# Attention in front of two MoE layers on one core: scores ahead of the v products, earlier stores of x, moved weight splits

## The chip, the cores and the metric

The kernel runs on one core of a Trainium2 chip, in one launch. The metric is the device time of that launch in microseconds. Names of engines: PE is TensorE, DVE VectorE, ACT ScalarE, POOL GpSimd, and SP the engine that issues the loads and stores (SPq its DMA queue). A round or a tile is given by its number n, a layer of the program by its name.

## What is computed

A recurrent attention with a decay w per head and channel, over 4 batches, 8 heads of 48 channels and 768 steps, feeds a mixture of 8 experts (one expert per token), and that a second, dense layer with the function h − tanh(h).

```python
def _attn_ref(r, k, v, w, u):                    # r, k, v: 4, 8, 768, 48
    for t in range(S):
        cur = np.einsum('bhd,bhe->bhde', u[None] * kt, vt)
        y[:, :, t] = np.einsum('bhd,bhde->bhe', rt, state + cur)
        state = w[None, :, :, None] * state + np.einsum('bhd,bhe->bhde', kt, vt)

def _moe_ref(x, w_gate, w1, w2):                 # x: 3072 x 384, F 1024
    expert_idx = np.argmax(x @ w_gate, axis=1)   # gate_w: its softmax value
    out[mask] = gate_w[mask, None] * (np.maximum(x[mask] @ w1[e], 0.0) @ w2[e])

def _moe2_ref(x, w_in, w_out):                   # 384 x 2048, 2048 x 384
    h = x @ w_in
    return (h - np.tanh(h)) @ w_out
```

## The kernel before

The attention is cut into 24 tiles of 128 steps: 6 chunks c of the sequence, 4 batches b in each, tile n = 4c + b. The loop `for n in range(NN + 1)` runs a round for each tile and one more. The order of the instructions on each engine is the order in which the program writes them; nothing reorders them later. Loads run three tiles ahead into five buffers (`t_b` holds r and k by channel, `n_b` holds r, k, v by step).

A round n does this. VectorE: `diag_sum(n+1)` (dt, L356) reduces GpSimd's product rku; `scale(n+1)` (L328) multiplies the two halves of t by tables of powers of w, one of them in PSUM (prkK) and the other, from tile 4 on, in SBUF (PRK); `mask(n)` (L377) copies the scores that lie below the diagonal from PSUM into `am`; `state_add(n)` (L402) adds the new keys' products to the state Sc. TensorE: the product of the state with tile n−1 (L418) and of `am` with its values (L423, "v products", both in `outp(n-1)`), the products for the state (`state_mm`, L390), and `scores(n)` (L372), which go into two PSUM banks A0 and A1, of which there is one pair. ScalarE: the copies of y (L428) and `diag(n+1)` (L363, eight parts), which writes the diagonal of `am` from dt. GpSimd: `side(n+2)` with the products rk (L336) and rku (L342), `side_kh(n+2)` (L351), whose keys only the state products use, and sw (L401).

Every fourth round has a piece of the routing for a whole chunk besides: `logits(c)` in round 4c+5 (lps on TensorE, lt on ScalarE), `gate` one round later, `rank_of`, `rank_in` (ohh, ol) and `rank_q` (hv on GpSimd) after that, then `idx_mm` and idf. Once a tile's gate is known, `xout_t` turns it back to rows of tokens (Xps, L570) and `xout_g` scales it on ScalarE (xs, L577) and stores it to xd. Xps and lps share one PSUM bank, "X", until round 23, when a second joins it. `XOUT` says which tiles leave in which round where that isn't n−7; in a list of two, the second follows the scores.

Between these stand the first weights of the MoE: `LOADS` says in which round a weight is loaded, `SPLITS` in which it is split into two parts for the matmuls: a cast on ScalarE (L84), then a subtraction on VectorE (L85). `head_end` (L492, five small VectorE operations) counts the first 256 tokens of expert 0 among chunks 0 to 3, that is tiles 0 to 15; `head_gather` (L597) fetches their rows from xd by the indices idxh with two indirect DMAs, and `head_trans` (L610) transposes them on TensorE behind the last v products. A barrier follows, and then the two MoE layers.

Of the kernel before, what the change touches and what calls it, by code (L numbers as in the profile page):

```python
# [8 lines left out]
F32 = mybir.dt.float32  # L9
# [5 lines left out]
ACTF = mybir.ActivationFunctionType  # L15
# [15 lines left out]
def rwkv_moe_moe_kernel(ctx: ExitStack, tc: tile.TileContext, rk_t, rkv, pk, u, wp1, wp2, out):  # L31


    nc = tc.nc
    B, C, P, _, H, D = rkv.shape
    N, DM = out.shape
    NT = N // P
    HP = H // 2
# [14 lines left out]
    H0 = C - 2  # L53
# [293 lines left out]
        side_rku(n)  # L347

    def side_kh(n):
        kh = kh_b[n % 3]  # L350
        nc.gpsimd.tensor_tensor(out=kh[:, R0:].rearrange("p (h d) -> p h d", d=D), in0=n_b[n % NB][:, 1], in1=KT, op=ALU.mult)  # L351
        st["kh", n] = kh
# [3 lines left out]
        nc.vector.tensor_reduce(out=dt, in_=st.pop(("rku", n)), axis=AX.X, op=ALU.add)  # L356
        st["dt", n] = dt

    def diag(n):
        dt = st.pop(("dt", n))  # L360
        am = at3.tile([P, 2, HP, P], F32, tag="am", name="am")
        for h in range(H):
            nc.scalar.activation(out=am[:, h % 2, h // 2, :], in_=ident, func=ACTF.Copy, scale=dt[:, h:h + 1])  # L363
        st["am", n] = am

    def scores(n):
        t = t_b[n % NB]
        ps = [ps1.tile([P, HP, P], F32, tag=f"A{q}", name=f"A{q}") for q in range(2)]
        for j in range(HP):
            for q in range(2):  # L370
                rows = slice(64, PT) if q else slice(0, 64)
                nc.tensor.matmul(ps[q][:, j, :], lhsT=t[rows, 1, j, :], rhs=t[rows, 0, j, :], start=True, stop=True)  # L372
        st["A", n] = ps

    def mask(n):
        for q, ps in enumerate(st.pop(("A", n))):
            nc.vector.copy_predicated(out=st["am", n][:, q],  # L377
                                      mask=mlt.bitcast(U32).unsqueeze(1).to_broadcast([P, HP, P]),
                                      data=ps)
# [25 lines left out]
        state_mm(n)  # L405
        state_add(n)

    def outp(n):
        c, b = seq[n]
        am = st.pop(("am", n))  # L410

        if c > 0:
            for i in range(2):
                for g in range(2):
                    for q in range(2):
                        rows = slice(64, PT) if q else slice(0, 64)
                        j, p0 = 2 * i + g, 64 * g
                        nc.tensor.matmul(Yp[q][p0:p0 + D, i, :], lhsT=Sc[c % 2][b][rows, j, :],  # L418
                                         rhs=t_b[n % NB][rows, 0, j, :], start=(i == 0), stop=False)
        for q in range(2):  # L420
            for j in range(HP):
                i, p0 = j // 2, 64 * (j % 2)
                nc.tensor.matmul(Yp[q][p0:p0 + D, i, :], lhsT=n_b[n % NB][:, 2, 2 * j + q, :],  # L423
                                 rhs=am[:, q, j, :], start=(c == 0 and i == 0), stop=(i == 1))
        if b == 0:
            st["y", c] = yp.tile([P, HP, B, P], F32, tag="y", name="y")
        for q in range(2):
            nc.scalar.copy(out=st["y", c].rearrange("p (q i) b t -> p q i b t", q=2)[:, q, :, b, :], in_=Yp[q])  # L428
# [280 lines left out]
    with tc.manual_schedule():  # L709
# [36 lines left out]
        k_table()  # L746
        side(1)
        nc.gpsimd.memset(cum[0], 0.0)
        LAG = 7
        L = C - 1  # L750
        LOADS = {5: (0, 0), 9: (0, 1), 13: (1, 0), 15: (1, 1), 17: (2, 0), 20: (2, 1), NN - 1: (3, 0)}
        SPLITS = {8: (0, 0), 12: (0, 1), 16: (0, 2), 18: (0, 3), **{NN - 3 + k: (1, k) for k in range(3)}}
        LATER = {0: ((3, 0), (3, 1)), 1: ((2, 2), (2, 3)), 2: ((3, 2), (3, 3))}
        XOUT = {NN - 3: (NN - 10, NN - 9), NN - 2: (), NN - 1: (NN - 8, NN - 7), NN: ()}
        for n in range(NN + 1):
            if n == NN:
                w_split(1, 3)
                w_split(2, 0)
                w_split(2, 1)
            if n + 3 < NN:  # L760
                load(n + 3)
            if n in LOADS:
                w_load(*LOADS[n])
            if n + 1 < NN:
                diag_sum(n + 1)
                scale(n + 1)
            at_step(n, 2, logits)
            at_step(n, 6, rank_q)
            xs_of = [m for m in XOUT.get(n, (n - LAG,)) if m >= 0]
            with_logits = n % B == 1 and n > B  # L770
            if n == NN - 1:
                st["both"] = True
            if xs_of and not with_logits:
                xout_t(xs_of[0])
            if 1 <= n <= NN:
                outp(n - 1)
                at_step(n, 6, rank_row)
            if n > 1 and n < NN:
                state_mm(n)
            if xs_of and with_logits:  # L780
                xout_t(xs_of[0])
            if xs_of:
                xout_g(xs_of[0])
            if 0 < n < NN - 1:
                diag(n + 1)
            if n < NN:
                scores(n)
                for m in xs_of[1:]:
                    xout_t(m)
                    xout_g(m)  # L790
                mask(n)
                if n == 0:
                    k_rows()
                    diag(1)
                elif n == 1:
                    state(0)
                    state(1)
                else:
                    state_add(n)
            if n + 2 < NN:  # L800
                side(n + 2)
                if n == 0:
                    side_kh(0)
                    side_kh(1)
                side_kh(n + 2)
            at_step(n, 3, logits2)
            at_step(n, 3, gate)
            at_step(n, 6, idx_mm)
            if n == H0 * B + 3:
                head_count()  # L810
            at_step(n, 4, rank_mm)
            at_step(n, 4, rank_of)
            at_step(n, 5, rank_in)
            if n == H0 * B + 3:
                head_end()
            if n == NN - 2:
                head_gather()
            if n == 0:
                keep_warm(8)
                gate_rows()  # L820
            if n == 1:
                scale_rows()
                gate_cols()
                nc.vector.tensor_reduce(out=nok, in_=ok, axis=AX.X, op=ALU.add)
                nc.vector.memset(one, 1.0)
            if n == 3:
                range_flag(ok)
                nc.vector.tensor_copy(out=e8p, in_=e8)
                nc.vector.tensor_copy(out=thp, in_=thr)
                for t in exs:  # L830
                    nc.vector.memset(t[:, :, E:E + 1], 1e-9)
                nc.vector.tensor_reduce(out=sel, in_=ident.rearrange("p (j x) -> p x j", j=HP)[:, 0:E, :],
                                        axis=AX.X, op=ALU.add)
            if n in SPLITS:
                w_split(*SPLITS[n])

# [675 lines left out]
```

## Time and profile before

| What | us |
|---|---|
| median of 3 runs (lowest, highest) | 772.84 (772.15, 774.85) |
| the profiled execution | 772.78 |
| span of its trace | 771.1 |
| PE busy in the span | 755.7 (98%) |
| DVE busy | 639.2 (83%) |
| ACT busy | 509.1 (66%) |
| POOL busy | 430.9 (56%) |

The profile is of one execution. Times in its rows are counted from the start of the span; what is outside it is 1.7 us. A row of the timeline gives the start, the duration, the engine and the line, the output and inputs, how many instructions were joined in the row, and in brackets how long the engine had been idle before and what ended that. The attention part ends at about 131 us.

### The profile page before, as it was taken

To read this page: it belongs to the slowest core of one execution; us is meant where nothing else is said; L and a number is where in the kernel's file an instruction comes from. 1 tells how busy PE (TensorE), PEld (TensorE's weight loads), DVE (VectorE), ACT (ScalarE), POOL (GpSimd) and SP (SyncE) were. 2 spreads that over 40 slices of the span, in tenths; PEclk is the share of its full clock that TensorE was granted. 3 is DMA by queue.
4 is the path that set the end of the run, shared out by engine and by line. 5 is a ranking of instruction groups with operands and counts; after the bars stand their busy time and mean duration, and the time that the engine had idled before them with its cause. 6 is when DMAs were issued, how large, how long until landed. Compare 5 with 4: busy or idle time off the path is not lost.

```text
span 771.1 us, 14624 instructions
## 1 busy us (share of the span) xinstructions
PE 755.7 (98%) x5200; PEld 684.6 (89%) x5200; DVE 639.2 (83%) x1155; ACT 509.1 (66%) x1091; POOL 430.9 (56%) x435
## 2 busy tenths in 40 slices
PE   8899989999999999999999999999999999999997
PEld 7688868998999999999898998989989989899887
DVE  7899996788899888964898888888888888888893
ACT  6788885464454445554887766776777677677881
POOL 6989952385877876765355353443534344343433
PEclk9999999999999999999999999999999999999999
DMA  8999945466999899974000010000001000000101
GB/s 238 261 291 290 318 128 167 145 189 201 256 230 271 223 305 286 250 198 144 1 1 0 1 42 1 0 21 21 1 1 42 1 1 24 18 1 1 41 1 42
DMA packets 34656, 89.67 MB, mean 116 GB/s; under 512 B 5499, under 2 KB 12704, under 8 KB 34578
## 3 DMA queue, kind: packets, MB, share of 16 engines
q1 hardware_dynamic: 30384, 78.68, 34.8%
q0 software_dynamic: 4192, 9.99, 4.6%
q8 instruction: 43, 0.70, 0.4%
q14 instruction: 35, 0.29, 0.1%
q10 hardware_dynamic: 2, 0.00, 0.0%
HBM read 72.92 MB, written 15.74 MB: 115 GB/s over the span
## 4 chain that ended last, share of the span: by engine, by line
PE 51%; issue 2%; ACT 1%; POOL 1%; POOLq 0%
PE h L1346 25%; PE o L1394 24%; PE y L1119 1%; PE hps L1094 1%; POOL out_dram L1407 0%; PE o L1346 0%; POOL g L1383 0%; POOLq L1453 0%; POOL xb L1383 0%; ACT s L1354 0%; ACT mk L1356 0%; POOLq L1507 0%; ACT xb L1382 0%; ACT z L1350 0%; ACT t L1352 0%
## 5 line engine op out<-in xcount | busy, mean ns | idle before, releaser
L1383 POOL TENSOR_TENSOR g<-t,g 128x512 fp32r<-128x512 f32 x93 | 120.3, 1294 | 178.6 <-ACT g L1382 128.5
L1346 PE MATMUL h<-xb,ring 128*128 128x512 f32 x855 | 213.6, 395 | 0.0
L1394 PE MATMUL o<-ring,g 128*128 128x384 f32 x1116 | 209.3, 336 | 0.0
L1394 PEld LDWEIGHTS o<-ring,g 128*128 128x128 f32 x1116 | 196.1, 188 | 8.2
L1346 PEld LDWEIGHTS h<-xb,ring 128*128 128x128 f32 x855 | 159.7, 188 | 30.5
L85 POOL TENSOR_TENSOR ring<-stg,ring 128x384 fp32r<-128x384 f32 x102 | 105.3, 1053 | 53.8 <-ACT ring L84 42.4
L1350 ACT ACTIVATE z<-h 128x512 f32<-128x512 f32 x95 | 56.9, 599 | 95.2 <-PE h L1346 95.2
L1119 PE MATMUL y<-h,ring 128*128 128x256 f32 (+7 forms) x576 | 114.2, 342 | 0.6 <-DVE h L1098 0.6
L1094 PE MATMUL hps<-xt,ring 128*128 128x472 f32 (+6 forms) x504 | 105.6, 353 | 0.1
L1119 PEld LDWEIGHTS y<-h,ring 128*128 128x128 f32 x576 | 101.3, 188 | 4.1 <-DVE h L1098 1.0
L1362 DVE TENSOR_TENSOR t<-t,h 128x512 f32<-128x512 f32 x95 | 65.1, 685 | 41.3 <-ACT t L1352 40.9
L1094 PEld LDWEIGHTS hps<-xt,ring 128*128 128x128 f32 x504 | 90.6, 188 | 3.7 <-DVEq L1233 0.4
L1367 DVE COPY_PREDICATED t<-mk,h 128x512 f32<-128x512 uint32 x95 | 71.4, 751 | 10.1 <-DVE h L1365 0.5
L84 ACT CAST ring<-stg 128x384 fp32r<-128x384 f32 x152 | 70.2, 512 | 9.5 <-DMA stg<-in_wp_dram 8.9
L1364 DVE SCALAR_TENSOR_TENSOR h<-s,h 128x512 f32<-128x512 f32 x95 | 66.2, 697 | 10.6 <-ACT g L1382 0.9
L1097 ACT ACTIVATE h<-hps 128x256 fp32r<-128x256 f32 (+7 forms) x64 | 32.1, 501 | 63.8 <-PE hps L1094 61.8
L1354 ACT ACTIVATE s<-z,gb 128x512 f32<-128x512 f32 x96 | 69.6, 725 | 0.0
L1356 ACT ACTIVATE mk<-z,gt 128x512 f32<-128x512 f32 x96 | 69.3, 721 | 0.0
L1365 DVE SCALAR_TENSOR_TENSOR h<-z,h 128x512 f32<-128x512 f32 x95 | 66.1, 696 | 3.3
L1363 DVE TENSOR_TENSOR h<-h,z 128x512 f32<-128x512 f32 x95 | 65.9, 693 | 0.0
L1382 ACT CAST g<-t 128x512 fp32r<-128x512 f32 x93 | 57.6, 619 | 9.7 <-DVE t L1367 7.8
L363 ACT ACTIVATE am<-ident,dt 128x128 f32<-128x128 f32 x192 | 58.6, 392 | 3.8 <-DVE dt L356 3.8
(254 smaller groups left out, 1039.6 us busy)
## 6 DMA issues: line engine op xcount, KB each, us to landing
stg<-in_wp_dram SPq DMA_DIRECT2D x64, 384.0 KB, 4.9
n<-in_rkv_dram SPq DMA_DIRECT2D x24, 576.0 KB, 6.0
d<-in_wp_dram SPq DMA_DIRECT2D x32, 384.0 KB, 5.8
t<-in_rk_t_dram SPq DMA_DIRECT2D x24, 384.0 KB, 7.1
wdec<-dcf SPq DMA_DIRECT2D x32, 192.0 KB, 5.3
xd<-xs SPq DMA_DIRECT2D x24, 192.0 KB, 3.9
stg<-wdec SPq DMA_DIRECT2D x12, 384.0 KB, 4.3
wl<-wdec SPq DMA_DIRECT2D x2, 768.0 KB, 6.0
```

Of the source, the lines that this page charges most:

```text
L84: nc.scalar.copy(out=dst[:, 0, sl], in_=of)
L85: eng.tensor_tensor(out=dst[:, 1, sl], in0=of, in1=dst[:, 0, sl].bitcast(F32), op=ALU.subtract)
L1094: nc.tensor.matmul(ps, lhsT=wf(a, kk), rhs=xt[e][b][:, kk, :], start=(n == 0), stop=(n == 8))
L1119: nc.tensor.matmul(yps[d], lhsT=wf(a)[:, d * P:(d + 1) * P], rhs=h2[:, b, :], start=(f == 0 and n == 0), stop=(f == CH1 - 1 and n == 2))
L1346: nc.tensor.matmul(ps, lhsT=wf(a, kk), rhs=xb[j][:, b, kk, :], start=(n == 0), stop=(n == 8))
L1354: nc.scalar.activation(out=s, in_=z, func=ACTF.Square, scale=G_K ** 0.5, bias=gb)
L1356: nc.scalar.activation(out=mk, in_=z, func=ACTF.Relu, scale=-1.0, bias=gt2)
L1364: nc.vector.scalar_tensor_tensor(out=ps, in0=s, scalar=G_K * G_D, in1=ps, op0=ALU.add, op1=ALU.mult)
L1365: nc.vector.scalar_tensor_tensor(out=ps, in0=z, scalar=G_A, in1=ps, op0=ALU.subtract, op1=ALU.mult)
L1367: nc.vector.copy_predicated(out=t, mask=mk.bitcast(U32), data=ps)
L1383: nc.gpsimd.tensor_tensor(out=g[:, 1, :], in0=ww, in1=g[:, 0, :].bitcast(F32), op=ALU.subtract)
L1394: nc.tensor.matmul(ops[q], lhsT=gg[i][:, b, q * P:(q + 1) * P], rhs=wf(a), start=(f == 0 and n == 0), stop=(f == CH2 - 1 and n == 2))
```

## The change

- Rounds 0 to 4 (`AHEAD = B + 1`): `scores(n)` and `mask(n)` stand ahead of the v products of tile n−1, and five of the eight parts of `diag(n+1)` ahead of the copies of y. `outp` is divided for it into `outp_state` and `outp`.
- `side_kh` returns at once for the last chunk, tiles 20 to 23.
- `SPLITS`: (0,0), (0,1), (0,2) one round later; (0,3) and (1,0) on GpSimd, in rounds 20 and 21.
- `XOUT`: tiles 12 and 13 leave in round 19, 14 and 15 in round 20.
- `head_end` in round 21 instead of 19; the load (2,1) in round 21 instead of 20.

```diff
     def side_kh(n):
+        if seq[n][0] == C - 1:
+            return
-    def diag(n):
-        dt = st.pop(("dt", n))
-        am = at3.tile([P, 2, HP, P], F32, tag="am", name="am")
-        for h in range(H):
-            nc.scalar.activation(out=am[:, h % 2, h // 2, :], in_=ident, func=ACTF.Copy, scale=dt[:, h:h + 1])
-        st["am", n] = am
+    def diag(n, part=range(H)):
+        if 0 in part:
+            st["am", n] = at3.tile([P, 2, HP, P], F32, tag="am", name="am")
+        dt, am = st["dt", n], st["am", n]
+        for q, j in (divmod(k, HP) for k in part):
+            h = 2 * j + q
+            nc.scalar.activation(out=am[:, q, j, :], in_=ident, func=ACTF.Copy, scale=dt[:, h:h + 1])
-        LAG = 7
+        LAG, AHEAD = 7, B + 1
-        LOADS = {5: (0, 0), 9: (0, 1), 13: (1, 0), 15: (1, 1), 17: (2, 0), 20: (2, 1), NN - 1: (3, 0)}
-        SPLITS = {8: (0, 0), 12: (0, 1), 16: (0, 2), 18: (0, 3), **{NN - 3 + k: (1, k) for k in range(3)}}
+        LOADS = {5: (0, 0), 9: (0, 1), 13: (1, 0), 15: (1, 1), 17: (2, 0), 21: (2, 1), NN - 1: (3, 0)}
+        SPLITS = {9: (0, 0), 13: (0, 1), 17: (0, 2), 20: (0, 3, nc.gpsimd), 21: (1, 0, nc.gpsimd), 22: (1, 1), 23: (1, 2)}
-        XOUT = {NN - 3: (NN - 10, NN - 9), NN - 2: (), NN - 1: (NN - 8, NN - 7), NN: ()}
+        XOUT = {NN - 5: (NN - 12, NN - 11), NN - 4: (NN - 10, NN - 9), NN - 3: (), NN - 2: (), NN - 1: (NN - 8, NN - 7), NN: ()}
...
-            if 1 <= n <= NN:
+            if n:
+                outp_state(n - 1)
+            if n < AHEAD:
+                scores(n)
+                mask(n)
+                if n:
+                    diag(n + 1, range(5))
+            if n:
                 outp(n - 1)
...
-                diag(n + 1)
+                diag(n + 1, range(5 if n < AHEAD else 0, H))
             if n < NN:
-                scores(n)
+                if n >= AHEAD:
+                    scores(n)
                 for m in xs_of[1:]:
                     xout_t(m)
                     xout_g(m)
-                mask(n)
+                if n >= AHEAD:
+                    mask(n)
...
-            if n == H0 * B + 3:
+            if n == NN - 3:
                 head_end()
```

TensorE, round 4 and the start of round 5, before (A_569 and A_570 are the scores of tile 4, `am,n_133` the v products of tile 3, kh_159 the state products of tile 4, lps the logits of chunk 0; repeated rows left out):

```order
L423 MATMUL yh_161<-am,n_133 48x128 x4
L423 MATMUL yh_162<-am,n_133 48x128 x4
L390 MATMUL yh_163<-n_134,kh_159 64x48
...
L372 MATMUL A_569<-t_129 128x128
L372 MATMUL A_570<-t_129 128x128
...
L452 MATMUL lps<-y,wgp 32x512 x4
```

The same place in the changed kernel, where the scores are A_542 and A_543:

```order
L375 MATMUL A_542<-t_129 128x128
L375 MATMUL A_543<-t_129 128x128
...
L428 MATMUL yh_161<-am,n_133 48x128 x4
L428 MATMUL yh_162<-am,n_133 48x128 x4
L393 MATMUL yh_163<-n_134,kh_159 64x48
...
L457 MATMUL lps<-y,wgp 32x512 x4
```

The scores of tile 4 moved from behind the state products to the head of the round; the logits follow the round as before.

ScalarE, rounds 20 and 21, before (xs is x of a tile, am the eight diagonals, lt the logits, rh a piece of the ranks):

```order
L428 COPY y<-yh_162 128x2x128
L577 ACTIVATE xs<-Xps,gt 128x384
L363 ACTIVATE am<-ident,dt 128x128 x8
L455 COPY lt<-lps 128x512
L428 COPY y<-yh_161 128x2x128
L428 COPY y<-yh_162 128x2x128
L546 ACTIVATE rh<-hv,pid 128x4x32
L577 ACTIVATE xs<-Xps,gt 128x384
L363 ACTIVATE am<-ident,dt 128x128 x8
L577 ACTIVATE xs<-Xps,gt 128x384
L84 CAST ring_70<-stg 128x384
```

The same rounds in the changed kernel:

```order
L433 COPY y<-yh_162 128x2x128
L582 ACTIVATE xs<-Xps,gt 128x384
L367 ACTIVATE am<-ident,dt 128x128 x8
L582 ACTIVATE xs<-Xps,gt 128x384
L84 CAST ring_69<-stg 128x384
L460 COPY lt<-lps 128x512
L433 COPY y<-yh_161 128x2x128
L433 COPY y<-yh_162 128x2x128
L551 ACTIVATE rh<-hv,pid 128x4x32
L367 ACTIVATE am<-ident,dt 128x128 x8
L84 CAST ring_70<-stg 128x384
```

Round 20 now has an x on either side of its diagonals and the cast of split (0,3) ahead of the logits' copy; round 21 has no x.

VectorE, the end of round 8 and of round 9, before (ohh and ol are of `rank_in`, idf the indices, ring the split):

```order
L527 TENSOR_TENSOR ohh<-sm,q_79 128x16
L530 TENSOR_TENSOR ol<-iotaf,sm 128x512
L85 TENSOR_TENSOR ring_69<-stg,ring_69 128x384
L356 TENSOR_REDUCE dt<-rku 128x8
...
L402 TENSOR_TENSOR Sc_148<-sw,yh_163 112x192
L556 COPY idf<-sm 128x32
L356 TENSOR_REDUCE dt<-rku 128x8
```

The same place in the changed kernel:

```order
L532 TENSOR_TENSOR ohh<-sm,q_79 128x16
L535 TENSOR_TENSOR ol<-iotaf,sm 128x512
L358 TENSOR_REDUCE dt<-rku 128x8
...
L405 TENSOR_TENSOR Sc_148<-sw,yh_163 112x192
L561 COPY idf<-sm 128x32
L85 TENSOR_TENSOR ring_69<-stg,ring_69 128x384
L358 TENSOR_REDUCE dt<-rku 128x8
```

The split moved from behind ol to behind idf, one round later.

## Rows read from the trace of the kernel before

**Rows 1.** Windows; columns: length, busy of PE, PEld, DVE, ACT, POOL, clock, DMA:

```profile
28.24:31.65 3.41, 3.41 (x42) 3.12 (x39) 2.56 (x11) 2.42 (x9) 3.33 (x4) 0.50 1.02 260
51.54:86.04 34.50, 34.35 (x604) 27.87 (x604) 33.95 (x84) 30.38 (x95) 31.82 (x35) 1.00 0.97 301
130.90:751.00 620.10, 619.33 (x3273) 570.16 (x3274) 515.67 (x838) 401.67 (x778) 325.73 (x292) 1.00 0.31 91
```

**Rows 2.** Timeline, TensorE, rounds 4 and 5; columns: start, duration, what, idle before:

```profile
27.86 1.71 PE L423 MATMUL yh<-am,n 128*48 128x128 f32 x16 [1.70 <-DVE am L377]
29.33 1.04 PE L390 MATMUL yh<-n,kh 128*64 128x48 f32 x16
30.29 1.80 PE L372 MATMUL A<-t 64*128 64x128 f32 x16
...
33.60 1.08 PE L423 MATMUL yh<-am,n 128*48 128x128 f32 x16
...
35.05 1.16 PE L372 MATMUL A<-t 64*128 64x128 f32 x16
```

**Rows 3.** Timeline, VectorE, rounds 3 to 5:

```profile
24.54 0.55 DVE L356 TENSOR_REDUCE dt<-rku 128x8 f32<-128x384 f32 x1 [0.56 <-POOL rku L342]
...
27.00 1.33 DVE L377 COPY_PREDICATED am<-mlt,A 128x512 f32<-128x512 uint32 x2
...
30.14 0.73 DVE L328 TENSOR_TENSOR t<-t,PRK 112x512 f32<-112x512 f32 x1
32.19 1.36 DVE L377 COPY_PREDICATED am<-mlt,A 128x512 f32<-128x512 uint32 x2 [1.32 <-PE A L372]
...
36.31 1.35 DVE L377 COPY_PREDICATED am<-mlt,A 128x512 f32<-128x512 uint32 x2 [0.50 <-PE A L372]
```

**Rows 4.** Timeline, VectorE, rounds 8 to 10:

```profile
51.07 0.55 DVE L85 TENSOR_TENSOR ring<-stg,ring 128x384 fp32r<-128x384 f32 x1
...
52.59 1.26 DVE L328 TENSOR_TENSOR t<-t,PRK 112x512 f32<-112x512 f32 x1
...
55.29 0.17 DVE L556 COPY idf<-sm 128x32 f32<-128x32 f32 x1
...
56.44 1.24 DVE L328 TENSOR_TENSOR t<-t,PRK 112x512 f32<-112x512 f32 x1
```

**Rows 5.** Timeline, ScalarE, diag(10) in round 9:

```profile
52.77 2.44 ACT L363 ACTIVATE am<-ident,dt 128x128 f32<-128x128 f32 x8
```

**Rows 6.** Timeline, VectorE, rounds 18 to 22:

```profile
95.96 0.81 DVE L85 TENSOR_TENSOR ring<-stg,ring 128x384 fp32r<-128x384 f32 x1
...
101.80 0.52 DVE L497 TENSOR_TENSOR bump<-ident,bump 128x1 f16<-128x1 f32 x1
...
108.16 1.34 DVE L377 COPY_PREDICATED am<-mlt,A 128x512 f32<-128x512 uint32 x2
...
110.62 0.56 DVE L85 TENSOR_TENSOR ring<-stg,ring 128x384 fp32r<-128x384 f32 x1 [0.53 <-ACT ring L84]
```

**Rows 7.** Timeline, ScalarE, x of tile 13 in round 20:

```profile
101.42 0.59 ACT L577 ACTIVATE xs<-Xps,gt 128x384 f32<-128x384 f32 x1
```

**Rows 8.** Timeline, TensorE, rounds 20 and 21:

```profile
99.84 1.26 PE L423 MATMUL yh<-am,n 128*48 128x128 f32 x16 [0.91 <-DVE am L377]
...
102.12 1.06 PE L452 MATMUL lps<-y,wgp 128*32 128x512 f32 x8
103.12 0.65 PE L418 MATMUL yh<-t,Sc 64*48 64x128 f32 x16
```

**Rows 9.** Timeline, TensorE, behind the last tile:

```profile
118.90 0.30 PE L610 MATMUL hp<-ident,n 128*128 128x128 f32 x1 [0.51 <-PE yh L423]
119.84 0.77 PE L610 MATMUL hp<-ident,n 128*128 128x128 f32 x5 [0.64 <-DMA n<-xd,idxh]
```

**Rows 10.** Timeline, GpSimd, the second gather of the head:

```profile
115.45 0.96 POOL L599 DMA_INDIRECT n<-xd,idxh  x1 [0.30 <-issue]
```

**Rows 11.** Timeline, GpSimd, rku(12) in round 10:

```profile
57.20 1.34 POOL L342 TENSOR_TENSOR rku<-rk,ub 128x384 f32<-128x384 f32 x1
```

More of the change, by code (lines that the diff above doesn't have):

```diff
@@ L406, in state, with outp_state @@
         state_add(n)
-    def outp(n):
+    def outp_state(n):
         c, b = seq[n]
-        am = st.pop(("am", n))
         if c > 0:
@@ L419, in outp @@
                                          rhs=t_b[n % NB][rows, 0, j, :], start=(i == 0), stop=False)
+    def outp(n):
+        c, b = seq[n]
+        am = st.pop(("am", n))
         for q in range(2):
```

## Prediction

> **What bounds the kernel now.** I read the stretches first [rows 1]. From 130.9 to 751 us TensorE is busy for 619.33 of 620.10 us: the two MoE layers are its own, the change touches nothing in them, and they begin only when the attention part is through. So whatever the attention part gains or loses moves the end by the same amount. Inside the attention part, VectorE is the full engine: 33.95 of 34.50 us between 51.54 and 86.04. A round there is a chain on VectorE (row sums dt, two scalings, mask, state, and a piece of gating every fourth round), and time is won only by taking work or waits off that chain, or off what it waits for. The third stretch, 28.24 to 31.65 us, is the one place with a low granted clock, 0.50, which is 1.2 instead of 2.4 GHz; it follows a TensorE idle time of 1.70 us [rows 2].
>
> The waits on VectorE [rows 3] say what paces the first rounds. In round 3 (24.54) it waits 0.56 for GpSimd's rku, and the rounds before begin in the same way: no order on TensorE helps there. In round 4 it waits 1.32 us for the scores, and in round 5 another 0.50. These two are what the first part of the change can reach. TensorE's rows of the same place [rows 2] show the other side: from 27.86 on there is no wait in front of any row through scores(5) at 35.05. TensorE is not waiting there, it is behind.
>
> **Part A: scores and mask ahead of the v products, rounds 0 to 4.** In round 4 scores(4) now stand before v(3). They read t(4), scaled by 27.0, but write the two PSUM banks that mask(3) reads, one pair only, and that mask runs from 27.00 to 28.33 [rows 3]. So TensorE now starts round 4 at 28.33 instead of 27.86, 0.47 later, with the same work queued behind it. mask(4) gains: scores(4) end at 28.33 + 1.80 = 30.13, before VectorE has scaled t(5) at 30.14 + 0.73 = 30.87, so the 1.32 us are gone and mask(4) runs at 30.87. But the next mask needs scores(5), which stand behind v(3), the state products, logits(0), v(4) and its state products, the same list as before: 36.31 + 0.47 = 36.78 instead of 36.31. The 1.32 us are given back one round later, as a wait of some 2 us for scores(5). I book **+0.4 us**.
>
> The lower bound is the case in which the clock stays full. v(3), the state products and scores(4) took 1.71 + 1.04 + 1.80 at half clock; v(4) and scores(5) at full clock took 1.08 and 1.16 [rows 2], so the three would save about 1.7 us. Not all of that arrives: logits(0) need y(3), whose copies on ScalarE now stand behind five parts of diag(5) (5/8 of the 2.44 us of a whole diagonal [rows 5], begun when dt(5) is there, half a microsecond ahead of the scaling at 30.14: until 31.2). With that, logits(0) end at about 32.7 and scores(5) at 35.9: −0.4. The upper bound, a half-clock stretch that reaches into logits(0) as well, is +1.0. I take the value near the upper side of zero because the idle stretch before round 4 keeps about its size (round 3 holds the same work as before, and its end and the start of round 4 both move back by some 0.4), and that is the one that the clock fell after. Rounds 1 to 3 stay at GpSimd's pace. v(0) to v(3) end about a microsecond later, so loads 5 to 8 are issued later; the DMA share there is 1.02 [rows 1], so the queue is not empty and they land as before.
>
> **Part B: three splits one round later (8→9, 12→13, 16→17).** Same instructions, another neighbour. In round 8 the split took 0.55 at 51.07; its ScalarE cast had been done since before. In round 9 VectorE is through with idf at 55.29 + 0.10, while ScalarE finishes diag(10) at 52.77 + 2.44 = 55.21 [rows 4, 5] and only then casts (about 0.5): VectorE waits 0.3 to 0.5 us. The nearest row is 110.62, where a split waited 0.53 for its cast in the same arrangement [rows 6]. Against that, VectorE reaches the scaling of round 9 earlier by the 0.47 that the split took, and that scaling took 1.26 because GpSimd held it up; free, it takes 0.73. A part of the 0.53 comes back. I take +0.23 in each of three cycles: **+0.7 us**, with bounds of −0.3 (all comes back) and +3.0 (rival 2).
>
> **Part C: rounds 18 to 24.** Off VectorE go split(0,3), 95.96 to 96.69, and split(1,0) with its wait, from 110.09 to about 111.1 [rows 6]; five small operations of head_end move from round 19 to 21 (the longest takes 0.52, at 101.80, and the five some 0.9). If VectorE alone decided, 1.7 us would be won. But x of tiles 13, 14 and 15 now follow each other through one PSUM bank ("X"), and ScalarE empties it behind its diagonals. Round 20: dt(20) starts at 95.96, where the split stood, and takes half a microsecond; diag(20) takes 2.44 more, to 99.1, and xs(13) 0.59 [rows 7], to 99.7. Only then can Xps(14) start, and behind it stand the state products (0.65 at 103.12) and v(19) (1.26 at 99.84) [rows 8]: v(19) start at 100.85, a microsecond later than now, where a free VectorE would have had mask(19) ready about as much earlier. scores(20) end at 103.05, and with head_end out of the way mask(20) runs at 103.1, about 1 us sooner than before. Round 21: xs(14) runs 102.35 to 102.95, diag(21) to 105.3, xs(15) to 105.8. logits(4) want the same bank, so they start at 105.85 instead of 102.12, and the state products, v(20) and scores(21) stand behind them: 106.85, 107.45, 108.5 to 109.65. mask(21) runs at 109.7 instead of 108.16 [rows 6]: **+1.5**. Then head_end (some 0.9) comes instead of split(1,0) (1.0 with its wait), and mask(22) and mask(23) stay 1.35 late.
>
> The tail gives it back. TensorE waits 0.51 and 0.64 us around its first transposes of the gathered rows (118.90 and 119.84) [rows 9], because the second gather, at 115.45 [rows 10], lands then, 4.4 later. In the new order x(15) is stored by 106 us, so the gathers wait for nothing but GpSimd: split(1,0) behind its cast (about 112.5 + at most 1.34, the longest GpSimd row of that size [rows 11]), so 113.7 and 115.1, landing by about 119.5. v(23) ended at 118.90 − 0.51 = 118.39 and end now at 119.74: the landing is hidden, and the transposes (0.30 + 0.77) run on behind v(23) to 120.8, where they ended at 119.84 + 0.77 = 120.6. Part C: **+0.2 us**. The lower bound is −2.2: the bank holds nobody up, VectorE's 1.01 of split(1,0) stays won, and the tail's 0.51 + 0.64 come on top. The upper bound is +1.4: the delay of the masks arrives and the tail gives nothing back.
>
> Without a price: kh(20) to kh(23) on GpSimd are removed, and two splits of about 1 us each are put there. GpSimd has room in the tail (it idles before the gathers) and nothing waits for it in rounds 20 and 21 but hv(3), whose products stand behind scores(21) anyway. w_load(2,1) goes out a round later on SP, behind nothing, and its halves are split only after the last round.
>
> **The sum.** 0.4 + 0.7 + 0.2 = +1.3 us. The profiled execution took 772.78 us, the median is 772.84; 772.84 + 1.3 = **774.1 us**.
>
> **Rival 1, faster.** TensorE keeps its full clock in round 4, the three splits cost nothing, and the bank chain does not bind, because dt(21) and with it diag(21) and xs(15) come some 2 us earlier than I have them: −0.4 + 0 − 2.2 = −2.6, 770.2 us. For it: every single step takes something off VectorE, the engine that is full. Against it: ScalarE's order puts xs(13) and xs(15) behind a diagonal of 2.44 us, whatever VectorE does.
>
> **Rival 2, slower.** A scaling with both inputs in SBUF takes 0.73 when GpSimd is quiet and 1.24 or 1.26 when it is not, and GpSimd's rku 1.34 beside it (57.20) [rows 4, 11]: one waits for the other. In round 10 VectorE asks at 56.44, ahead of rku at 57.20, and so wins the place. If the wait for the cast in round 9 makes it ask 0.77 us later or more, rku goes first and VectorE waits for all of it: about 1.0 more in each of the three cycles. 0.4 + 3.0 + 0.2 = +3.6, 776.4 us. It decides at that point alone: which of the two starts first in rounds 10, 14 and 18. The Trainium skill says in "SBUF — State Buffer", section "Who interferes with whom", that VectorE with two SBUF inputs contends with a reading GpSimd instruction, that the first to issue holds the shared pair of ports for its whole instruction, and that the other stands still. By that rule it would be all or nothing here; the rows 1.24, 1.26 and 1.34 agree that both lose, but show no whole block.
>
> **Rival 3, no change.** The full clock in round 4 (−0.4), splits at no cost, part C as booked (+0.2): −0.2, 772.6 us.
>
> **How the numbers follow.** Forecast 0.38, rival 1 0.28, rival 2 0.20, rival 3 0.14. A measurement of this kernel tells 0.3% from no change, 2.3 us: faster is under 770.5, slower over 775.2. Rival 1 lies just beyond that, its own spread (769.7 to 770.8) puts 0.22 of 0.28 there, and 0.02 come from rival 3's lower side. Slower are all of rival 2 and 0.03 of the forecast. Faster 0.24, within 0.53, slower 0.23. The range goes from −3.1 (rival 1 with part B at −0.3 and a little more in the tail), 769.7, to rival 2's 776.4. The forecast's own range is 772.6 to 775.4.
>
> **What would show it.** Right: VectorE's wait before mask(4) gone and one of about 2 us before mask(5); TensorE's clock low again for a stretch near 28 to 32 us; a wait of 0.3 to 0.5 us before the split in round 9; logits(4) starting only after xs(15), near 106 us; no wait between v(23) and the gathered rows' transposes; the last barrier near 132 us instead of 130.9. Wrong: mask(5) before 36 us (part A), scalings over 2 us in rounds 10, 14, 18 (rival 2), or logits(4) before 104 us (rival 1).

## The result: slower by half a per cent

The changed kernel takes 778.54 us (median of 20 runs, 773.66 to 781.09), the kernel before 774.07 (20 runs, 771.32 to 778.74). The ratio is 1.0053, with a 95% interval of 1.0035 to 1.0070: 4.1 us slower, between 2.7 and 5.4. That is over the 0.3% that the text ahead took as the bound, and its 774.1 us for a kernel of 772.84 foresaw +1.3. The side of the change was right, the size was a third of what was measured. By the ratio the forecast kernel would stand at 776.9, above the 776.4 that ended the stated range, and the text ahead had given most of the chance (0.53) to no measurable change. The profiled execution of the changed kernel has a span of 777.7 us, 6.6 more than the 771.1 of the kernel before: these two executions lie further apart than the medians do, so the rows below show more than the loss of the medians.

VectorE's timeline of the changed kernel shows the places that the prediction spoke of (columns: start, duration, what, how many; in brackets the idle time before and what ended it; these rows answer to [rows 3], [rows 4] and [rows 6]):

```profile
35.33 1.35 DVE L380 COPY_PREDICATED am<-mlt,A 128x512 f32<-128x512 uint32 x2 [1.23 <-ACT am L367]
...
50.21 0.55 DVE L358 TENSOR_REDUCE dt<-rku 128x8 f32<-128x384 f32 x1
...
54.89 1.22 DVE L85 TENSOR_TENSOR ring<-stg,ring 128x384 fp32r<-128x384 f32 x1 [0.80 <-ACT ring L84]
...
66.15 0.55 DVE L358 TENSOR_REDUCE dt<-rku 128x8 f32<-128x384 f32 x1 [1.54 <-POOL rku L342]
...
75.59 1.03 DVE L85 TENSOR_TENSOR ring<-stg,ring 128x384 fp32r<-128x384 f32 x1 [1.54 <-ACT ring L84]
...
93.84 0.94 DVE L85 TENSOR_TENSOR ring<-stg,ring 128x384 fp32r<-128x384 f32 x1 [0.56 <-ACT ring L84]
94.71 0.54 DVE L358 TENSOR_REDUCE dt<-rku 128x8 f32<-128x384 f32 x1
...
108.11 1.34 DVE L380 COPY_PREDICATED am<-mlt,A 128x512 f32<-128x512 uint32 x2 [2.23 <-PE A L375]
...
115.85 1.35 DVE L380 COPY_PREDICATED am<-mlt,A 128x512 f32<-128x512 uint32 x2 [3.45 <-PE A L375]
```

The same two round starts in the kernel before:

```profile
51.54 0.55 DVE L356 TENSOR_REDUCE dt<-rku 128x8 f32<-128x384 f32 x1
...
90.80 0.54 DVE L356 TENSOR_REDUCE dt<-rku 128x8 f32<-128x384 f32 x1
```

Read the rows against the starts of the rounds, the sum dt of the next tile. Round 9 begins at 50.21 instead of 51.54, 1.33 us early; 0.47 of that is the split, which the kernel before has done by then and the changed one has not. Three moved splits later round 18 begins at 94.71 instead of 90.80, 3.9 us late. Each split now waits for its cast, 0.80, 1.54 and 0.56 us, and each takes 1.22, 1.03 and 0.94 instead of the 0.55 of [rows 4]. At the end mask(20) and mask(21) wait 2.23 and 3.45 us for scores.

TensorE of the changed kernel, rounds 20 and 21 and behind the last tile (they answer to [rows 8] and [rows 9]):

```profile
103.10 0.66 PE L575 MATMUL Xps<-ident,y 128*128 128x128 f32 x4 [1.31 <-ACT xs L582]
...
104.72 1.95 PE L428 MATMUL yh<-am,n 128*48 128x128 f32 x16
...
110.42 1.85 PE L457 MATMUL lps<-y,wgp 128*32 128x512 f32 x8 [1.82 <-ACT xs L582]
...
125.73 0.84 PE L615 MATMUL hp<-ident,n 128*128 128x128 f32 x6
```

Xps(14) waits for xs(13) and logits(4) for xs(15), both on ScalarE, as the order said. The transposes of the gathered rows follow the last v products without a wait, where [rows 9] had 0.51 and 0.64. The first matmul behind the barrier starts at 136.99; it was 130.91 before, and the two MoE layers are as they were (TensorE busy for 251.00 of 251.00 us between 500 and 751 in both).

The granted clock of three stretches (columns: length, busy of PE, PEld, DVE, ACT, POOL, clock, DMA share, GB/s; the second row answers to the first of [rows 1]):

```profile
14.30:18.40 4.10, 3.98 (x32) 3.54 (x34) 3.42 (x7) 2.53 (x9) 4.02 (x6) 0.58 0.76 186
28.24:31.65 3.41, 2.59 (x44) 1.77 (x41) 3.38 (x6) 2.81 (x10) 2.89 (x4) 1.00 1.01 240
102.00:114.00 12.00, 9.07 (x88) 5.82 (x90) 8.03 (x18) 6.06 (x17) 6.07 (x7) 0.72 0.60 190
```

Near 28 us the clock is now full. It is low in round 1, where TensorE had waited 1.46 us for mask(0) to free the score banks (14.29), and again in rounds 20 and 21, behind the waits for xs: v(19) took 1.95 us and the logits 1.85, where [rows 8] show 1.26 and 1.06.

```profile
14.29 2.63 PE L375 MATMUL A<-t 64*128 64x128 f32 x16 [1.46 <-DVE am L380]
```

### The profile page after: what moved, and what is told of

It is laid out like the page before. It is cut to its first block, busy times and chain, and to the rows that moved or that the text cites. A ratio compares the mean times of both kernels' runs of the same rounds, so it can differ in the third digit from the quotient of the medians.

```text
span 777.7 us, 14615 instructions
## 1 busy us (share of the span) xinstructions
PE 758.6 (98%) x5200; PEld 685.8 (88%) x5200; DVE 637.5 (82%) x1153; ACT 509.4 (65%) x1091; POOL 428.0 (55%) x433
## 4 chain that ended last, share of the span: by engine, by line
PE 51%; issue 2%; ACT 1%; POOL 1%; POOLq 0%
PE h L1360 25%; PE o L1408 23%; PE y L1133 1%; PE hps L1108 1%; POOL out_dram L1421 0%; PE o L1360 0%; POOL g L1397 0%; POOLq L1467 0%; POOL xb L1397 0%; ACT s L1368 0%; ACT mk L1370 0%; POOLq L1521 0%; ACT xb L1396 0%; ACT z L1364 0%; ACT t L1366 0%
## 5 line engine op out<-in xcount | busy, mean ns | idle before, releaser
L85 POOL TENSOR_TENSOR ring<-stg,ring 128x384 fp32r<-128x384 f32 x104 | 108.4, 1063 | 60.6 <-ACT ring L84 48.2
```

Source lines behind the costliest of these rows:

```text
L85: eng.tensor_tensor(out=dst[:, 1, sl], in0=of, in1=dst[:, 0, sl].bitcast(F32), op=ALU.subtract)
```

## The experiments

Three theories stood at the start. SPLITS: the moved splits lose time behind ScalarE's diagonals. BANK: x of tiles 13 to 15 and logits(4), through one PSUM bank, cost more than the tail gives back. LOADS: the later v products free the buffers later, the loads fall behind, and later rounds pay. Each ratio below is to the kernel before, run on the same chip, with its 95% interval; the changed kernel stands at 1.0053. Two kernels are compared by their ratios, and such a difference is uncertain by about 0.25 to 0.35%. A trace is of one execution, which can lie several us from the median of its kernel; where that matters, the text says so.

### One part undone, or one part alone

**Scores behind the v products again.**

```diff
-        LAG, AHEAD = 7, B + 1
+        LAG, AHEAD = 7, 0
```

> The changed kernel with scores and mask behind the v products again in all rounds; the rest of the change stays. The changed kernel stands at 1.0053 of the kernel before. Theory LOADS (v products come later, buffers are freed later, the DMA queue runs dry near 16 to 20 us, and later rounds wait for the values of their tile): most of the loss goes, ratio 1.000 to 1.001, no row products on GpSimd waiting for a load by more than 1.0 us. Theory SPLITS (the cast behind the diagonals): 1.005, waits before the splits of rounds 9, 13, 17 stay at 0.5 to 1.5 us. Theory BANK (x of tiles 13 to 15 and logits(4) share a bank behind the diagonals): 1.005, and the waits of 2.2 and 3.5 us before mask(20) and mask(21) stay.

Measured: 1.0073 (1.0046 to 1.0101), 778.39 us. LOADS falls in the form stated: without the first part the kernel is no faster. It does not follow that late loads cost nothing: two products on GpSimd still wait more than 1.0 us for a load here (1.42 and 1.03), and the account of the prediction comes back to them. In its trace the DMA share between 12 and 20 us is 0.74, lower than the 0.87 of the changed kernel, so a thin DMA queue there is not the mark of that part either.

**The three splits back.**

```diff
-        SPLITS = {9: (0, 0), 13: (0, 1), 17: (0, 2), 20: ...
+        SPLITS = {8: (0, 0), 12: (0, 1), 16: (0, 2), 20: ...
```

> The changed kernel with splits (0,0), (0,1), (0,2) back in rounds 8, 12 and 16. LOADS: 1.004 to 1.005, the waits for loads stay, since what VectorE saves is given back to them. SPLITS: the three waits (0.80, 1.54, 0.56) and the longer splits (1.22, 1.03, 0.94 instead of 0.55) go, some 3.5 us: 1.001. BANK: 1.005.

Measured: 0.9994 (0.9970 to 1.0017), 774.03 us. Against 1.0053 this is 0.59%, 4.6 us (uncertain by 0.3%): the whole loss. The waits of the three moved splits (0.80 + 1.54 + 0.56) and their added length (3.19 − 3 × 0.55) come to 4.4 us, where the expectation has some 3.5; shorter scalings and other waits stand beside them (below), so that the two numbers meet is no full account. No split waits for its cast in this trace, and the lengths are 1.02, 0.55 and 0.55: the old place is no guarantee of the short length either. The waits before mask(20) and mask(21) stay, 3.04 and 1.51 us.

**x, head_end, the late load and the late splits back.**

```diff
-        XOUT = {NN - 5: (NN - 12, NN - 11), NN - 4: (NN - 10, NN - 9), NN - 3: (), ...
+        XOUT = {NN - 3: (NN - 10, NN - 9), ...
-            if n == NN - 3:
+            if n == H0 * B + 3:
                 head_end()
```

> The changed kernel with x of tiles 12 to 15, head_end, the load (2,1) and splits (0,3), (1,0) where they were before. LOADS: 1.004 to 1.005. SPLITS: 1.005. BANK: mask(20) and mask(21) wait no more than 0.3 us, the tail's 1.15 us come back: net some 3 us, 1.001 to 1.002.

Measured: 1.0041 (1.0022 to 1.0059), 776.15 us. Against 1.0053 this part costs 0.12%, with about 0.25% either way; LOADS and SPLITS expected that, BANK more. The waits before mask(20) and mask(21) are gone, as BANK had it, but not the loss.

**The first part alone, on the kernel before** (all other tables and head_end as before, kh for all tiles).

> The kernel before with only the first part of the change: scores and mask ahead of the v products and the diagonals in two pieces in rounds 0 to 4. LOADS: slower, 1.002 to 1.004, with a DMA share of 0.8 to 0.9 near 16 to 20 us. SPLITS and BANK: no loss from this part, 0.998 to 1.000, since round 11 began 1.3 us earlier in the changed kernel before the first moved split.

Measured: 1.0025 (1.0008 to 1.0041), 774.52 us. A small loss, as LOADS had it. It doesn't come back in the other pairs (below), so I do not build on it. (The lead of 1.3 us in the expectation is the one at the start of round 9.)

**The three splits alone, on the kernel before.**

> The kernel before with only the three splits moved, from rounds 8, 12, 16 to 9, 13, 17. SPLITS alone carry the loss: 1.004 to 1.007. If they cost only beside the other parts: under 1.003.

Measured: 1.0026 (1.0002 to 1.0050), 776.58 us. That is under what SPLITS expected and within the other branch, that the splits cost most beside the other parts; the interval reaches into both. Its trace is of the slowest of its twelve executions, 781.44 us. It shows shorter waits for the cast, and three splits at two to over three times the 0.55:

```profile
53.40 1.12 DVE L85 TENSOR_TENSOR ring<-stg,ring 128x384 fp32r<-128x384 f32 x1 [0.55 <-ACT ring L84]
...
74.63 1.79 DVE L85 TENSOR_TENSOR ring<-stg,ring 128x384 fp32r<-128x384 f32 x1 [0.30 <-ACT ring L84]
...
94.70 1.78 DVE L85 TENSOR_TENSOR ring<-stg,ring 128x384 fp32r<-128x384 f32 x1 [0.30 <-ACT ring L84]
```

The price of the move thus has four pairs: 0.59% (changed, splits back), 0.26% (before, splits moved), 0.83% (scores behind the v products, 1.0073, against the same without the moved splits, 0.9990 below) and, with kh differing besides, 0.16% (x and head_end back, 1.0041, against the first part alone, 1.0025). All are on one side, their mean is 0.46%, 3.6 us; each is uncertain by 0.25 to 0.35%, which the second barely clears and the fourth does not. If the 0.30% that kh is worth (below) is added to the fourth, it is 0.46% too.

### What makes the moved splits dear

**The cast ahead of the diagonals.** ScalarE casts at the head of the diagonals of rounds 9, 13 and 17; VectorE subtracts where the change has it.

```diff
+            if n in (9, 13, 17):
+                w_cast(*SPLITS[n])
             if 0 < n < NN - 1:
                 diag(n + 1, range(5 if n < AHEAD else 0, H))
```

> The changed kernel with the casts of rounds 9, 13 and 17 ahead of the diagonals on ScalarE, so that the subtraction on VectorE finds them done; it still stands beside GpSimd's products. WAIT (VectorE loses the time until the cast is there): 1.000 to 1.002, splits without a wait. PORT (the subtraction has both inputs in SBUF and loses to GpSimd's products, 0.9 to 1.8 us instead of 0.55): 1.003 to 1.005, and the splits stay at 0.9 to 1.8 us.

Measured: 0.9994 (0.9972 to 1.0017), 773.43 us. The loss is gone, with the subtraction in the same place: the place is dear only while the cast comes late. VectorE of this kernel:

```profile
53.10 0.72 DVE L93 TENSOR_TENSOR ring<-stg,ring 128x384 fp32r<-128x384 f32 x1
...
70.80 0.73 DVE L93 TENSOR_TENSOR ring<-stg,ring 128x384 fp32r<-128x384 f32 x1
...
88.55 0.73 DVE L93 TENSOR_TENSOR ring<-stg,ring 128x384 fp32r<-128x384 f32 x1
```

No wait, and also no 1.0 to 1.8 us: PORT's lengths went together with the wait. So this run alone does not separate the two, since a subtraction that starts earlier relative to GpSimd's products, or later, has another rest of them to sit out.

**One input in PSUM.** In the three splits a product of the cast with the table in PSUM, on 112 of 128 partitions, takes the place of the subtraction; the low parts of these weights are left out. A memset of 1.02 us on VectorE stands ahead of round 0 besides, where the kernel otherwise waits 1.47 us for GpSimd.

```diff
-        eng.tensor_tensor(out=dst[:, 1, sl], in0=of, in1=dst[:, 0, sl].bitcast(F32), op=ALU.subtract)
+        eng.tensor_tensor(out=dst[0:PT, 1, sl], in0=dst[0:PT, 0, sl].bitcast(F32), in1=PRKp[0]..., op=ALU.mult)
```

> The changed kernel with the subtraction of splits (0,0), (0,1) and (0,2) replaced by a product of the cast with a table in PSUM, over 112 of 128 partitions: the wait for the cast stays, one of the two inputs no longer lies in SBUF; the low parts of these weights are not computed. WAIT: 1.004 to 1.005, waits of 0.5 to 1.5 us as before. PORT: 1.000 to 1.002, each product at about 0.55 us.

Measured: 1.0020 (1.0004 to 1.0037), 775.62 us. VectorE:

```profile
52.86 0.55 DVE L86 TENSOR_TENSOR ring<-ring,prkK 112x384 fp32r<-112x384 f32 x1 [0.62 <-ACT ring L84]
...
70.96 0.56 DVE L86 TENSOR_TENSOR ring<-ring,prkK 112x384 fp32r<-112x384 f32 x1
...
89.37 0.56 DVE L86 TENSOR_TENSOR ring<-ring,prkK 112x384 fp32r<-112x384 f32 x1 [0.56 <-ACT ring L84]
```

The lengths are 0.55 and 0.56, as PORT had it. Of the waits only the first and the third stand, 0.62 and 0.56; the second is gone, so this run is no clean separation either: 1.2 us of waits are left of 2.9. From 1.0053 to 1.0020, 0.33%, 2.6 us, is what came back with the second SBUF input, directly and through the wait that went with it. The ratio is under the 1.004 of WAIT, but 1.7 us of waits went too; what speaks for PORT here is the lengths. What remains to 0.9994, 0.26%, 2.0 us, is uncertain by 0.28%: that the rest of the wait has a price of its own is read from the rows, and not shown by the times.

### The shared bank

**The early x without the first part and without the moved splits.**

> The changed kernel without its first part and with splits (0,0) to (0,2) back in rounds 8, 12, 16; what is left is the earlier x of tiles 12 to 15, no kh for the last chunk, the two splits on GpSimd and the moved head_end. With x of tiles 13 and 15 ahead of the diagonals besides, it stood at 0.9957. BANK: the wait of logits(4) for x(15) is back, 2 to 4 us before mask(20) and mask(21), ratio 0.999 to 1.001. If the bank is no matter: 0.995 to 0.997, and the gain is that of fewer GpSimd products and an earlier gather.

Measured: 0.9990 (0.9967 to 1.0013), 774.31 us. First TensorE, then VectorE of this kernel:

```profile
104.96 1.94 PE L457 MATMUL lps<-y,wgp 128*32 128x512 f32 x8 [2.07 <-ACT xs L582]
```

```profile
111.71 1.36 DVE L380 COPY_PREDICATED am<-mlt,A 128x512 f32<-128x512 uint32 x2 [4.77 <-ACT am L367]
```

**The same with x ahead of the diagonals on ScalarE in rounds 19 and 20.**

```diff
-            if 0 < n < NN - 1:
+            if 0 < n < NN - 1 and n not in (NN - 5, NN - 4):
                 diag(n + 1, range(5 if n < AHEAD else 0, H))
...
                     xout_g(m)
+                if n in (NN - 5, NN - 4):
+                    diag(n + 1)
```

> The changed kernel without its first part, with splits (0,0) to (0,2) back in rounds 8, 12, 16, and with x of tiles 13 and 15 ahead of the diagonals on ScalarE in rounds 19 and 20. BANK (the shared bank behind the diagonals costs what the tail gives back): logits(4) no longer wait, mask(20) and mask(21) wait under 0.5 us, 0.995 to 0.998. If the bank is no matter: 0.999 to 1.001.

Measured: 0.9957 (0.9937 to 0.9977), 769.93 us. Again TensorE, then VectorE:

```profile
100.90 1.06 PE L457 MATMUL lps<-y,wgp 128*32 128x512 f32 x8 [0.72 <-ACT xs L582]
```

```profile
104.75 1.35 DVE L380 COPY_PREDICATED am<-mlt,A 128x512 f32<-128x512 uint32 x2 [1.16 <-PE A L375]
```

The bank held behind the diagonals costs 0.33%, 2.6 us, with 0.3% either way; the kernels with the first part (next run, against the splits back) give 0.32% for the same exchange. The wait of logits(4) shrinks from 2.07 to 0.72, they run at full clock (1.06 instead of 1.94), and mask(21) waits 1.16 instead of 4.77. (The row of the 4.77 names the diagonals; those of tile 21 had ended at 104.44, and it is the scores, 109.74 + 1.87 = 111.61, that end the wait.) The 1.16 are more than the 0.5 that I expected of this kernel. The diagonals, which follow later now, delay nobody.

**The same with the first part of the change.**

> As the kernel at 0.9957, but with scores and mask ahead of the v products in rounds 0 to 4, as the change has them. If that part costs what it cost alone (1.0025): 0.997 to 0.999. If it is worth nothing on balance: 0.995 to 0.997. If it gains, as the comparison of 1.0053 with 1.0073 hints: 0.992 to 0.994.

Measured: 0.9962 (0.9940 to 0.9985), 771.07 us. With and without the first part: 0.9962 and 0.9957 here, 0.9994 and 0.9990 with the bank as changed and the splits back. Scores ahead of the v products are worth nothing that can be measured.

**kh of the last chunk alone left out of the kernel before.**

> The kernel before with one thing changed: no kh for tiles 20 to 23. If four GpSimd products of 1 us matter (fewer meetings with VectorE's scalings in rounds 18 to 21): 0.997 to 0.999. If they are off the path, as I booked them: 0.999 to 1.001.

Measured: 0.9970 (0.9949 to 0.9991), 772.04 us: a gain of 2.3 us (0.7 to 3.9) from four GpSimd products that nobody waits for. In the kernel before, one of them, kh(21), stands beside a scaling of VectorE; first GpSimd, then VectorE:

```profile
97.59 1.00 POOL L351 TENSOR_TENSOR kh<-n,KT 128x384 f32<-128x384 f32 x1
```

```profile
97.75 1.40 DVE L328 TENSOR_TENSOR t<-t,PRK 112x512 f32<-112x512 f32 x1
```

VectorE of the kernel without kh, to be read beside these and [rows 6], where the split took 0.81 at 95.96:

```profile
96.80 0.62 DVE L85 TENSOR_TENSOR ring<-stg,ring 128x384 fp32r<-128x384 f32 x1
...
98.41 0.68 DVE L328 TENSOR_TENSOR t<-t,PRK 112x512 f32<-112x512 f32 x1
```

The scaling behind it took 1.40 before and takes 0.68. Together 0.9 us. Where the rest of the 2.3 comes from this trace cannot show: it is of the slowest of the twelve executions, 775.33 us, slower than the profiled one of the kernel before.

**x ahead of the diagonals, and the moved splits with their casts ahead too.**

> As the kernel at 0.9957, but the three splits in rounds 9, 13, 17 with their casts ahead of the diagonals. If only the wait and the meeting with GpSimd made the moved splits dear: the same as in rounds 8, 12, 16, 0.994 to 0.997, splits of 0.55 to 0.75 us without a wait. If the place itself costs something: 0.998 or more.

Measured: 0.9942 (0.9916 to 0.9967), 770.68 us, the lowest ratio of all. Within 0.3%, rounds 9, 13 and 17 are as good a place for the splits as 8, 12 and 16, once the cast is there: in the trace they take 0.54, 0.73 and 0.72 without a wait. (That trace is of the slowest of its ten executions, 777.91 us. There xs(13) waits 3.10 us for an earlier store of x, Xps(14) 2.65 for xs(13), and mask(20) 3.55 for its scores: x ahead of the diagonals does not keep the bank free when a store is late.) Both this kernel and the one at 0.9957 beat the kernel before and the changed one; from each other they cannot be told.

## Why the prediction was wrong

**Part B was mis-sized, and it decided.** I booked +0.7 us for the three splits with an upper bound of +3.0; the undoing is worth 4.6 us in the changed kernel and 3.6 in the mean of the pairs. Two numbers of that step failed. The split was priced at its length in round 8, 0.55, where it started just ahead of GpSimd's rh (at 51.12, which then took 0.76 instead of 0.40); in round 9 it comes while GpSimd's products run and took 0.94 to 1.22, in other runs up to 1.82. [Rows 6] held the warning: the split at 95.96 took 0.81. The wait for the cast was put at 0.3 to 0.5; it was 0.80, 1.54 and 0.56. Rounds 9, 13 and 17 are just those in which ScalarE has a piece of the ranks (rh) ahead of x and the diagonals, and that needs hv of GpSimd; when GpSimd is late, the whole row behind it is, and the cast is the last. ScalarE of the changed kernel in round 13:

```profile
71.95 0.40 ACT L551 ACTIVATE rh<-hv,pid 128x128 f16<-128x128 f16 x1 [1.47 <-POOL hv L542]
72.25 0.56 ACT L582 ACTIVATE xs<-Xps,gt 128x384 f32<-128x384 f32 x1
72.72 2.44 ACT L367 ACTIVATE am<-ident,dt 128x128 f32<-128x128 f32 x8
75.05 0.50 ACT L84 CAST ring<-stg 128x384 fp32r<-128x384 f32 x1
```

The 1.47 us at the top come out as the 1.54 us that VectorE waits, until 75.59, for the cast at the bottom. GpSimd was late because of a load: ahead of hv it had rk, rku and kh to do, without a break, from 68.51 on.

```profile
68.51 1.01 POOL L336 TENSOR_TENSOR rk<-n 128x384 f32<-128x384 f32 x1 [0.96 <-DMA n<-in_rkv_dram]
```

And the credit that I took off, shorter scalings, came in full without helping. VectorE's groups between 46 and 98 us, first of the changed kernel, then of the kernel before (columns: line, what, count; busy us, mean ns; idle before):

```profile
L328 DVE TENSOR_TENSOR t<-t,PRK 112x512 f32<-112x512 f32 x11 | 8.9, 806 | 0.0
...
L358 DVE TENSOR_REDUCE dt<-rku 128x8 f32<-128x384 f32 x11 | 6.0, 546 | 1.7 <-POOL rku L342 1.7
...
L85 DVE TENSOR_TENSOR ring<-stg,ring 128x384 fp32r<-128x384 f32 x3 | 3.2, 1064 | 2.9 <-ACT ring L84 2.9
```

```profile
L328 DVE TENSOR_TENSOR t<-t,PRK 112x512 f32<-112x512 f32 x12 | 13.0, 1083 | 0.0
...
L356 DVE TENSOR_REDUCE dt<-rku 128x8 f32<-128x384 f32 x12 | 6.5, 543 | 0.0
```

The eleven scalings save 11 × 0.277 = 3.0 us, more than I credited. The same stretch holds 2.9 us of waits for casts, 3.2 − 3 × 0.55 = 1.5 of longer splits, and a wait that I did not have, 1.7 us for GpSimd's rku. GpSimd, too, waited for its tile's values in that stretch, six times and 4.3 us in all; the longest is 1.41 us at 57.90:

```profile
57.90 1.01 POOL L336 TENSOR_TENSOR rk<-n 128x384 f32<-128x384 f32 x1 [1.41 <-DMA n<-in_rkv_dram]
```

In the kernel before it waited for none there, with the splits back once (1.65), with the cast first twice (3.1), with one input in PSUM seven times (5.2). So a part of the waits in the profiled execution goes back to late loads, and how much of the loss they carry is not settled. Nor is it settled whether the loads were late because of the kernel: between 44 and 60 us the changed kernel's profiled execution moved 275 GB/s at a DMA share of 1.03, that of the kernel before 301 at 0.97.

**Rival 2 had the right mechanism at the wrong instruction.** It asked which of scaling and rku is first in rounds 10, 14 and 18, and gave 776.4. No scaling took 2 us there. The instruction that lost the place was the split itself, which I had written down as having the one length of its old neighbourhood. It has both inputs in SBUF, just as the scaling has. With one input in PSUM the length was 0.55 or 0.56 in all three places; with two it was 0.54 to 1.82 there, over all runs. The Trainium skill says in "SBUF — State Buffer", section "Who interferes with whom", that a VectorE instruction with two SBUF inputs contends with a GpSimd instruction that reads SBUF, and that one with at most one does not. The traces agree with that.

The prediction was wrong that 1.24, 1.26 and 1.34 show no whole block; it left out GpSimd's rk. First GpSimd of the kernel before, then GpSimd of the changed kernel beside the split at 54.89:

```profile
56.13 0.99 POOL L336 TENSOR_TENSOR rk<-n 128x384 f32<-128x384 f32 x1
57.20 1.34 POOL L342 TENSOR_TENSOR rku<-rk,ub 128x384 f32<-128x384 f32 x1
```

```profile
54.70 1.00 POOL L353 TENSOR_TENSOR kh<-n,KT 128x384 f32<-128x384 f32 x1
55.65 0.83 POOL L404 TENSOR_TENSOR sw<-Sc,pq 112x192 f32<-112x192 f32 x1
```

The scaling at 56.44 ends at 57.68; its own 0.68 (its length in a quiet place of the changed kernel) would begin at 57.00, when rk is all but through, and rku, which starts at 57.20, takes 1.34 instead of 1.00, as if it stood until the scaling ends. The split at 54.89 ends at 56.11; its own 0.55 would begin at 55.56, when kh is all but through, and sw then takes 0.83 instead of 0.51. So the rows fit a whole block: the length is the rest of the product that runs when VectorE asks, plus the instruction's own time. The longest lengths cover two GpSimd instructions (1.79 at 74.63 in the run with the splits alone: sw at 74.54 and rk, 75.01 to 76.00).

**kh was booked at nothing, and is a gain of 0.3%.** The step said that nothing waits for these products, which is true; it left out that they hold up VectorE's instructions in rounds 18 to 21 (scaling 1.40 to 0.68). By that price the gain hid part of the loss, and the changed kernel with kh would have been slower still; no run puts kh back.

**Part A: the sign of the local effect was wrong, the sum nearly right.** I expected the half clock near 28 to 32 us to stay and mask(5) at 36.78. The clock is full there, and mask(5) ran at 35.33, under the 36 that I had named as the sign of an error. The step that failed is that TensorE's idle stretch before round 4 keeps its size: it was 1.70 us and is 0.31, and TensorE starts the round at 26.75 and not at 28.33, because the v products fill it and mask(3) comes a microsecond sooner (the scaling ahead of it took 0.69 instead of 1.47).

```profile
26.75 1.76 PE L375 MATMUL A<-t 64*128 64x128 f32 x16 [0.31 <-DVE am L380]
...
34.07 1.16 PE L375 MATMUL A<-t 64*128 64x128 f32 x16
```

The wait did move to mask(5), as 1.23 us instead of 2: it ends with scores(5), 34.07 + 1.16 = 35.23 (the row names the diagonals, but those of tile 5 had ended at 31.89). The low clock moved to round 1, where TensorE now waits for the score banks; VectorE waits 0.59 us more there for the state products, and had that to spare (dt(3) starts at 20.66, where it waited for GpSimd until 20.74). The bound of −0.4 was too narrow: round 9 began 1.33 us early, 0.86 of it without the split. Nor do the loads quite land as before: the DMA share from 12 to 20 us is 0.87 and was 1.02. Yet in time the part is worth +0.05% and +0.04% in two pairs, +0.25% alone, and −0.20% in the changed kernel (1.0053 against 1.0073). What eats its lead I have not shown.

**Part C: the mechanism was right step by step.** logits(4) waited for xs(15), the gathers came right behind split(1,0) on GpSimd (118.19, then 119.36 and 121.12), and the tail's waits vanished. (The five operations of head_end take 1.0 us in the kernel before, 101.41 to 102.43, and not 0.9.) The kernel with the early x but neither of the other parts, 0.9990, against that without kh alone, 0.9970, makes the part +0.2% ± 0.3%, 1.5 us, where I had +0.2 us. What I missed is that TensorE's clock falls behind the two waits: 0.72 from 102 to 114 us, where the kernel before had 1.00, and the products behind them at up to twice their length. Rival 1's condition (the bank doesn't bind) can nearly be had by one exchange in ScalarE's order. That kernel, which has no part A and its splits where they were, stands at 0.9957; the 770.2 us of rival 1 are 0.9966.

## What to carry to other kernels

When an instruction is moved, price it in its new neighbourhood: a VectorE operation with both inputs in SBUF is as long as GpSimd's work beside it allows (0.54 to 1.82 us here for the same subtraction), and its producer's place in the other queue decides whether it waits. Move the producer with it; here the cast ahead of eight diagonals undid a loss of 0.6%, and x ahead of them gained another 0.3%. An instruction that nobody waits for can still cost time, by what it holds up on another engine (a scaling of 0.68 took 1.40 here); leave it out if its result is not used.

## What was not expected of the hardware

A wait of TensorE on the bank cost more than its own length, though not each time. In the changed kernel waits of 1.31 and 1.82 us were followed by the half clock, and the logits' matmuls took 1.85 us instead of 1.06. With the splits back, a wait of 1.27 us before Xps(14) was followed by it too (scores(20) took 2.08 us instead of 1.16). The same wait of 1.27 in the kernel without the first part and without the moved splits was not (scores(20) took 1.16); there the clock fell behind the next wait, 2.07 us (logits 1.94). Waits of 0.36 and 0.72 us (x ahead of the diagonals) were followed by full-clock rows. What makes the difference between the two waits of 1.27 is not shown.

The removal of four GpSimd products of about 1 us, off every chain of waits, gained 2.3 us (0.7 to 3.9), of which only 0.9 could be found in VectorE's rows.
